# Cluster similarities with the tokens as stationary operand, and the softmax reciprocals turned in another step

## The chip, the cores and the metric

The kernel runs on one core of one Trainium2 chip. The metric is the device time of one execution in microseconds (us). The engines run at the same time, each through its own queue in program order: TensorE (PE in the profile, its loads of stationary operands PEld), VectorE (DVE), ScalarE (ACT), GpSimd (POOL) and SyncE (SP), which here only issues DMAs. They wait for each other through semaphores.

## The reference

An attention in which a query sees the keys of its own cluster alone, and two dense layers behind it:

```python
B, H, S, D = 2, 8, 768, 64          # 16 centroids a head
q_assign = argmax(q_n @ c_n)        # cluster of each query, by normalised centroids
k_assign = argmax(k_n @ c_n)        # cluster of each key
mask   = q_assign[:, :, :, None] == k_assign[:, :, None, :]
scores = where(mask, q @ k.T / 8, -1e9)
attn   = softmax(scores) @ v        # then (1536, 512)
x = gelu_like(attn @ w_in) @ w_out  # 512 -> 2048 -> 512
x = relu(x @ w_in2)**2 @ w_out2     # 512 -> 2048 -> 512
```

Inputs are float32, and every product is made of float32r parts (a high and a low part), so that the argmax and the result are exact enough.

## The kernel before

**Stages.** Attention comes first, then the two dense layers. The change touches the attention alone.

**Attention.** The 16 pairs of batch and head are worked in eight groups of two heads. A head has six tiles of 128 queries, so a group has twelve steps and the main loop (L528) has 96 tiles. The loop makes the scores of a tile two steps (LEAD) before it uses them. A step of a group is numbered u = 0 to 11.

**A step** issues, in this order: the scores on PE (L346, L347: four matmuls into one of two PSUM tiles "big0", "big1"), the row maximum on DVE (L352), the turns of an older tile's exponentials on PE (L370: two halves of three transpositions into "pt0" and "pt1"), the high part of each half on ACT (L380), the low part on DVE (L383), a share of the product with v on PE (L395), the exponential on ACT (L361), and then the side work for the next group. Each engine keeps this order.

**Side work** (`side`, L500) prepares the next group while this one is worked: `split` makes high and low parts of q and k (a cast on DVE, a subtraction on POOL), `turn` transposes them on PE (L240) into the PSUM bank "sd", `turned` copies them out on ACT (L251) and sends a half to other partitions by a DMA of SP (L256). The heads of k and q are split in steps 5, 8 and 10 and in step 0, the turns stand in steps 7, 9, 10, 11 and 0 to 3. Steps 4 and 5 make the similarities, step 6 `best` and `bested`, step 7 `hot`, step 8 `rows` and `rowed`. Nearly all of this side work passes through the bank "sd".

**Similarities.** `cpad` holds the centroids' columns padded with zeros to 64 and 128, so that four accumulating matmuls (L264) give the similarities of both heads of q and k, high and low part of the centroids, as 128 rows of 384 tokens; ACT copies them out (L271), and `best` (L277) multiplies them by two stacked identities (`ident2`), which turns them to tokens by rows and adds the high and the low part. `bested` takes the maximum over the 16 clusters (L283), compares (L285), and weighs by the cluster's number (L288, on POOL); `hot` takes the maximum again (L294) and compares (L296, `hot_n`), so that the first of equal clusters wins. `rowed` sends the result to the operands of the scores by eight DMAs of SP (L322).

**Reciprocals.** After a group's last exponential `recip` (L423, L424) inverts the sums on DVE. `recip_rows` then transposes them on PE into "sd" (L429), DVE copies them out (L431, `rows`), and SP writes them to DRAM (L433). `spread` (L440) reads them back by two DMAs, each row on 64 partitions, and `norm` (L446) multiplies the group's result with them on POOL. They stand in step 0, step 2 and step 7 of the next group.

**Queues.** SP issues its DMAs in program order, about 0.6 us each, POOL works `split`'s low parts, `merged` (L418: adds the two halves of a product when their DMA has landed), `vals` and `norm` in program order.

Of the kernel before, what the change touches and what calls it, by code (L numbers as in the profile page):

```python
# [10 lines left out]
F32 = mybir.dt.float32  # L11
# [20 lines left out]
def tile_kernel(ctx, tc, q, k, v, cent, w_in1, w_out1, w_in2, w_out2, cw_cols, out):  # L32
# [101 lines left out]
    def attention(actx):  # L134
# [50 lines left out]
        cpad = one.tile([P, 2, H, 2, NS * C], F32R, name="cpad")  # L185
        nc.gpsimd.memset(f32(cpad), 0.0)

        ident2 = one.tile([P, NS * C], F32, name="ident2")
        nc.vector.tensor_copy(ident2[0:NS * C], identF[0:NS * C, 0:NS * C])
        nc.vector.tensor_copy(ident2[NS * C:], identF[NS * C:, NS * C:])  # L190
# [19 lines left out]
        def centroid_columns(c_hl):  # L210
            pc = psum([P, 2, H, C], F32R, "sd", "pc")
            for t in range(2):
                nc.tensor.transpose(pc[:, t].rearrange("p h c -> p (h c)"),
                                    c_hl[:, t].rearrange("p a d -> p (a d)"), identR)
            for x in range(2):
                for i in range(G):
                    o = C * (x * G + i)
                    nc.scalar.copy(cpad[:, x, i::G, :, o:o + C].rearrange("p h t c -> p t h c"),
                                   f32(pc[:, :, i::G, :]))


        class Prep:
# [35 lines left out]
            def sims(self, half, tag="sd"):  # L258

                self.ps = psum([P, QB], F32, tag, "ps")  # L260
                cols = slice(half * QB, (half + 1) * QB)
                both = [(x, hh) for x in (1, 0) for hh in range(G)]
                for x, hh in both:
                    nc.tensor.matmul(self.ps, cpad[:, x, self.h0 + hh].rearrange("p t c -> p (t c)"),  # L264
                                     self.__dict__["qk"[x] + "2", hh][:, cols],
                                     start=((x, hh) == both[0]), stop=((x, hh) == both[-1]))

            def simmed(self, half):
                if half == 0:
                    self.st = one.tile([P, S], F32, tag="st", name="st")  # L270
                nc.scalar.copy(self.st[:, half * QB:(half + 1) * QB], self.ps)  # L271

            def best(self):

                self.pm = psum([P, NJ, NS, C], F32, "sd", "pm")
                for j in range(NJ):
                    nc.tensor.matmul(self.pm[:, j].rearrange("p h c -> p (h c)"),  # L277
                                     self.st[:, j * P:(j + 1) * P], ident2, start=True, stop=True)

            def bested(self, start=False):  # L280
                pm = self.pm
                mx = tiny.tile([P, NJ, NS], F32, tag="mx", name="mx", bufs=1)
                nc.vector.tensor_reduce(out=mx, in_=pm, op=ALU.max, axis=AX)  # L283
                sim = one.tile([P, NJ, NS, C], F32, tag="sim", name="sim")
                nc.vector.tensor_tensor(  # L285
                    out=sim, in0=pm, in1=mx.unsqueeze(3).to_broadcast([P, NJ, NS, C]), op=ALU.is_equal)
# [177 lines left out]
        for half in range(2):  # L464
            p0.sims(half, ("sd", "pa")[half])
            p0.simmed(half)
        p0.best()
# [32 lines left out]
        def side(gn, u):  # L500
# [10 lines left out]
            elif u in (4, 5):  # L511
                pe, copy = (lambda: p.sims(u - 4)), (lambda: p.simmed(u - 4))
            elif u == 6:
                pe, copy = p.best, p.bested
            elif u == 7:
                mid = p.hot
            elif u == 8:
                pe, copy = p.rows, p.rowed
# [9 lines left out]
        for t in range(-LEAD, NTILE):  # L528
# [24 lines left out]
            if (t + LEAD) % GT == 0 and t > 0:  # L553
# [24 lines left out]
            if (t + LEAD) % GT == 2 and t > 0:  # L578
                spread((t + LEAD) // GT - 1)
            if t % GT == 5 and 0 < t // GT < NG:  # L580
# [177 lines left out]
```

## Time and profile before

| | us |
|---|---|
| median of 3 runs (820.99 to 822.8) | 822.67 |
| profiled execution | 823.47 |
| its span | 821.7 |
| PE busy in the span | 791.8 |
| DVE busy | 572.8 |
| ACT busy | 437.5 |
| POOL busy | 203.8 |

The span runs from the first instruction of the program to its last; the execution is a little longer. Busy PE time counts the pipeline of each matmul, so it does not tell what PE could do at its peak. The attention takes the first 290 us of the span, a third of it. In a list of waits a line tells which instruction had to wait, what released it, the sum, the number of such waits and the longest. In a timeline a row is an instruction, or several of one kind that follow each other; in brackets stands the idle time of the engine before it and what ended it.

### The profile page before, as it was taken

How to read it: one execution, taken by the hardware profiler on the slowest of the kernel's cores; microseconds unless marked ns; L12 is line 12 of the kernel's file. 1: busy time of each engine (PE TensorE's matmuls, PEld its weight loads, DVE VectorE, ACT ScalarE, POOL GpSimd, SP SyncE). 2: the span in 40 equal slices, each digit the busy share in tenths (PEclk: the TensorE clock that was granted, in tenths of full speed). 3: DMA queues.
4: the chain of work that ended last, by engine and by line, in shares of the span. 5: the costliest groups of instructions: out<-in, count | busy, mean ns of one | idle time of the engine just before them, and what ended most of it. 6: DMA issues, size and time to landing. Idle time of an engine off the chain costs nothing.

```text
span 821.7 us, 12438 instructions
## 1 busy us (share of the span) xinstructions
PE 791.8 (96%) x4610; PEld 696.6 (85%) x4610; DVE 572.8 (70%) x941; ACT 437.5 (53%) x925; POOL 203.8 (25%) x186
## 2 busy tenths in 40 slices
PE   5899999999998999999999999999999999999997
PEld 4789889889897888888888888878888888888886
DVE  7888798898889699999759999988322225222222
ACT  5788878888887745555535445464222224222222
POOL 3525344435336343333202233322000000000000
PEclk9799999999999999999999999999999999999999
DMA  9432523513211134444303344331000002000002
GB/s 247 138 80 71 140 45 107 138 41 112 69 35 42 44 103 128 128 129 127 104 4 115 113 129 129 119 112 52 1 0 1 1 1 77 0 1 1 1 1 77
DMA packets 40412, 60.89 MB, mean 74 GB/s; under 512 B 4224, under 2 KB 31648, under 8 KB 40352
## 3 DMA queue, kind: packets, MB, share of 16 engines
q1 hardware_dynamic: 35456, 53.03, 22.5%
q10 hardware_dynamic: 4896, 7.08, 2.6%
q8 instruction: 36, 0.59, 0.3%
q14 instruction: 24, 0.20, 0.1%
HBM read 46.18 MB, written 3.19 MB: 60 GB/s over the span
## 4 chain that ended last, share of the span: by engine, by line
PE 86%; DVE 8%; ACT 4%; issue 1%; ACTq 0%; POOL 0%; POOLq 0%; DVEq 0%
PE ph L129 32%; PE y L651 16%; PE y L642 10%; PE pa L395 6%; PE pt L370 6%; PE y L644 5%; PE ps L346 3%; PE ps L347 3%; ACT e L361 2%; DVE el L383 2%; DVE nm L352 2%; PE pt L240 2%; PE ps L264 1%; PE pm L277 1%; DVE dec L96 1%
## 5 line engine op out<-in xcount | busy, mean ns | idle before, releaser
L626 DVE TENSOR_TENSOR s<-s 128x512 f32<-128x512 f32 x64 | 36.2, 566 | 134.6 <-ACT s L625 134.6
L129 PE MATMUL ph<-xh,ih 128*128 128x512 f32 (+1 forms) x512 | 110.6, 338 | 1.4 <-ACT ih L102 1.2
L129 PE MATMUL ph<-xl,ih 128*128 128x512 f32 (+1 forms) x512 | 110.3, 337 | 0.5 <-DVE xl L117 0.4
L129 PE MATMUL ph<-xh,il 128*128 128x512 f32 (+1 forms) x512 | 109.6, 336 | 0.0
L352 DVE TENSOR_REDUCE nm<-ps 128x1 f32<-128x768 f32 x96 | 91.1, 949 | 23.4 <-PE ps L347 22.6
L630 ACT CAST gh<-s 128x512 fp32r<-128x512 f32 (+1 forms) x128 | 65.5, 512 | 75.0 <-DVE s L626 50.7
L383 DVE TENSOR_TENSOR el<-pt,eh 128x384 fp32r<-128x384 f32 x192 | 97.4, 548 | 7.4 <-ACT eh L380 6.8
L93 DVE SCALAR_TENSOR_TENSOR dec<-raw,dec 128x512 uint32<-128x512 uint32 x64 | 100.3, 1567 | 1.1
L625 ACT ACTIVATE s<-ph 128x512 f32<-128x512 f32 x64 | 31.2, 487 | 129.4 <-PE ph L129 129.4
L129 PEld LDWEIGHTS ph<-xh,ih 128*128 128x128 f32 x512 | 84.5, 188 | 17.0 <-ACT ih L102 1.9
L631 DVE TENSOR_TENSOR gl<-s,gh 128x512 fp32r<-128x512 f32 (+1 forms) x128 | 71.4, 557 | 39.4 <-ACT gh L630 39.4
L361 ACT ACTIVATE e<-ps,nm 128x768 f32<-128x768 f32 x96 | 88.4, 921 | 10.8 <-DVE nm L352 10.2
L380 ACT CAST eh<-pt 128x384 fp32r<-128x384 f32 x192 | 83.9, 493 | 19.2 <-PE pt L370 18.9
L129 PEld LDWEIGHTS ph<-xl,ih 128*128 128x128 f32 x512 | 83.3, 190 | 11.4 <-DVE xl L117 1.2
L129 PEld LDWEIGHTS ph<-xh,il 128*128 128x128 f32 x512 | 83.4, 190 | 10.0
L370 PE MATMUL pt<-identF,e 128*128 128x128 f32 x576 | 82.2, 277 | 3.8 <-DVE el L383 3.7
L103 POOL TENSOR_TENSOR il<-dec,ih 128x512 fp32r<-128x512 f32 x32 | 41.7, 1304 | 142.4 <-ACT ih L102 128.5
L79 ACT ACTIVATE dec<-raw 128x512 f32<-128x512 f32 x64 | 43.2, 676 | 61.5 <-DMA raw<-in_moe_w_out_dram 37.1
L651 PE MATMUL y<-oh,gh 128*128 128x512 f32 x192 | 75.1, 391 | 0.0
L651 PE MATMUL y<-ol,gh 128*128 128x512 f32 x192 | 75.1, 391 | 0.0
L651 PE MATMUL y<-oh,gl 128*128 128x512 f32 x192 | 74.7, 389 | 0.0
L346 PE MATMUL ps<-k,q 80*128 80x512 f32 x192 | 72.0, 375 | 1.9 <-ACT k L320 1.9
(118 smaller groups left out, 1535.7 us busy)
## 6 DMA issues: line engine op xcount, KB each, us to landing
raw<-in_moe_w_in_dram SPq DMA_DIRECT2D x32, 512.0 KB, 4.4
raw<-in_moe_w_out_dram SPq DMA_DIRECT2D x32, 512.0 KB, 3.3
k<-k SPq DMA_DIRECT2D x16, 192.0 KB, 2.8
q<-q SPq DMA_DIRECT2D x16, 192.0 KB, 2.5
rr<-row SPq DMA_DIRECT2D x16, 192.0 KB, 3.5
out_dram<-o SPq DMA_DIRECT2D x12, 256.0 KB, 2.3
both<-both SPq DMA_DIRECT2D x30, 96.0 KB, 2.1
rawk<-in_k_dram ACTq DMA_DIRECT2D x6, 384.0 KB, 3.3
```

Of the source, the lines that this page charges most:

```text
L93: nc.vector.scalar_tensor_tensor(out=t, in0=high, scalar=0xC0000000, in1=t, op0=ALU.bitwise_and, op1=ALU.bitwise_or)
L129: nc.tensor.matmul(ph, w[:, kc * P:(kc + 1) * P], xs[kc][z][:, a:a + n], start=(j == 0), stop=(j == len(terms) - 1))
L346: nc.tensor.matmul(ps[:, a:a + n], q1[0:K1, qs], k1[0:K1, a:a + n], start=True, stop=False)
L352: nc.vector.tensor_reduce(out=nm, in_=live["s", t], op=ALU.max, axis=AX, negate=True)
L361: nc.scalar.activation(e, live.pop(("s", t)), ACTF.Exp, bias=live.pop(("nm", t)), accum_out=sums[:, s:s + 1])
L370: nc.tensor.transpose(pt[:, i], e[:, kc * P:(kc + 1) * P], identF)
L380: nc.scalar.copy(place("eh", t, u), live["pt", t, u])
L383: nc.vector.tensor_tensor(out=place("el", t, u), in0=live.pop(("pt", t, u)), in1=f32(place("eh", t, u)), op=ALU.subtract)
L630: nc.scalar.copy(gh, self.s)
L631: nc.vector.tensor_sub(gl, self.s, f32(gh))
L642: nc.tensor.matmul(y[m], l[:, cs], gha if hi else gla, start=first, stop=last)
L651: nc.tensor.matmul(y[m], l[:, cs], r, start=(fc == 0 and z == 0), stop=(fc == KF - 1 and z == 2))
```

## The change

The similarities are computed with the tokens on the partitions. The 128 columns of tokens of q or k are the stationary operand, and the 16 columns of the head's centroids, high and low part side by side, stream past it: 12 matmuls of 32 columns for k in step 4 and 12 for q in step 5. ACT copies the high part's products out and DVE adds the low part's. `best`, the padded centroids, their memset and `ident2` are gone, and `bested` reads SBUF. At the start, for the first group, the same calls stand in the place of the old ones, so that the two adds come ahead of the first `decode` on DVE.

The transposition of the reciprocals with its copy and its DMA moves from step 0 to step 6, where the bank "sd" has no other use now, `spread` from step 2 to step 8, behind `rowed`, and `norm` from step 7 to step 10, behind that step's `split`. The last group's stay where they were.

```diff
-        cpad = one.tile([P, 2, H, 2, NS * C], F32R, name="cpad")
-        nc.gpsimd.memset(f32(cpad), 0.0)
-        ident2 = one.tile([P, NS * C], F32, name="ident2")
-        nc.vector.tensor_copy(ident2[0:NS * C], identF[0:NS * C, 0:NS * C])
-        nc.vector.tensor_copy(ident2[NS * C:], identF[NS * C:, NS * C:])
+        cols = one.tile([P, H, 2, C], F32R, name="cols")
...
-            for x in range(2):
-                for i in range(G):
-                    o = C * (x * G + i)
-                    nc.scalar.copy(cpad[:, x, i::G, :, o:o + C].rearrange("p h t c -> p t h c"),
-                                   f32(pc[:, :, i::G, :]))
+            nc.scalar.copy(cols.rearrange("p h t c -> p t h c"), f32(pc))
...
-            def sims(self, half, tag="sd"):
...
-            def simmed(self, half):
...
-            def best(self):
...
+            def sims(self, nm, tag="sd"):
+                self.ps = psum([P, NJ, G, 2, C], F32, tag, "ps")
+                for hh in range(G):
+                    for j in range(NJ):
+                        nc.tensor.matmul(self.ps[:, j, hh].rearrange("p t c -> p (t c)"),
+                                         self.__dict__[nm + "2", hh][:, j * P:(j + 1) * P],
+                                         cols[:, self.h0 + hh].rearrange("p t c -> p (t c)"), start=True, stop=True)
+
+            def summed(self, nm):
+                if nm == "k":
+                    self.sim = one.tile([P, NJ, NS, C], F32, tag="sim", name="sim")
+                at = G * (nm == "k")
+                dst = self.sim[:, :, at:at + G]
+                nc.scalar.copy(dst, self.ps[:, :, :, 0])
+                nc.vector.tensor_tensor(out=dst, in0=self.ps[:, :, :, 1], in1=dst, op=ALU.add)
 
             def bested(self, start=False):
-                pm = self.pm
+                sim = self.sim
...
-        for half in range(2):
-            p0.sims(half, ("sd", "pa")[half])
-            p0.simmed(half)
-        p0.best()
+        for i, nm in enumerate("kq"):
+            p0.sims(nm, ("sd", "pa")[i])
+            p0.summed(nm)
         tf = decode(*m0)
...
             elif u in (4, 5):
-                pe, copy = (lambda: p.sims(u - 4)), (lambda: p.simmed(u - 4))
+                pe, copy = (lambda: p.sims("kq"[u - 4])), (lambda: p.summed("kq"[u - 4]))
             elif u == 6:
-                pe, copy = p.best, p.bested
+                copy = p.bested
...
-            if (t + LEAD) % GT == 0 and t > 0:
+            if (t + LEAD) % GT == 6 and t + LEAD > GT or t == NTILE - LEAD:
                 recip_rows((t + LEAD) // GT - 1)
...
-            if (t + LEAD) % GT == 2 and t > 0:
+            if (t + LEAD) % GT == 8 and t + LEAD > GT:
                 spread((t + LEAD) // GT - 1)
-            if t % GT == 5 and 0 < t // GT < NG:
+            if t % GT == 8 and 0 < t // GT < NG:
                 norm(t // GT - 1)
```

## Rows read from the trace of the kernel before

**Rows 1.** The page's chain of waits: shares of the span by engine

```profile
PE 86%; DVE 8%; ACT 4%; issue 1%; ACTq 0%; POOL 0%; POOLq 0%; DVEq 0%
```

**Rows 2.** The list of waits, 21.5 to 275 us: sum, times, longest

```profile
PEld pt L240 <- issue: 9.2, 6, 1.5
...
PE pt L240 <- DVE rows L431: 7.2, 6, 1.2
```

**Rows 3.** The chain in order of time, step 0 of a group: start, length, what

```profile
120.59 0.20 DVE rows L431
```

**Rows 4.** Timeline of weight loads, one group: start, length, instruction, count, idle before

```profile
96.62 0.19 PEld L346 LDWEIGHTS ps<-k,q 80*128 80x128 f32 x1
...
101.21 0.36 PEld L264 LDWEIGHTS ps<-k,cpad 128*128 128x128 f32 x2
...
101.91 0.19 PEld L346 LDWEIGHTS ps<-k,q 80*128 80x128 f32 x1
...
103.33 1.42 PEld L277 LDWEIGHTS pm<-ident,st 128*128 128x128 f32 x12
104.67 0.19 PEld L346 LDWEIGHTS ps<-k,q 80*128 80x128 f32 x1
...
110.05 0.19 PEld L346 LDWEIGHTS ps<-k,q 80*128 80x128 f32 x1
...
111.30 0.31 PEld L370 LDWEIGHTS pt<-identF,e 128*128 128x128 f32 x3 [0.15 <-DVE el L383]
...
125.66 0.41 PEld L240 LDWEIGHTS pt<-identR,nat 128*128 128x128 f32 x3
```

**Rows 5.** Groups of weight loads, 0 to 290 us: count, busy us, mean ns, idle before

```profile
L240 PEld LDWEIGHTS pt<-identR,nat 128*128 128x128 f32 x192 | 23.4, 149 | 14.3 <-issue 9.2 <-DVE nat L233 1.4 <-POOL nat L233 1.1
L277 PEld LDWEIGHTS pm<-ident,st 128*128 128x128 f32 x96 | 12.1, 200 | 0.5 <-ACT st L271 0.5
L264 PEld LDWEIGHTS ps<-q,cpad 128*128 128x128 f32 x32 | 6.4, 206 | 0.0
```

**Rows 6.** Timeline of DVE, steps 6 to 8 of the same group

```profile
102.98 0.96 DVE L352 TENSOR_REDUCE nm<-ps 128x1 f32<-128x768 f32 x1 [0.60 <-PE ps L347]
103.86 1.01 DVE L383 TENSOR_TENSOR el<-pt,eh 128x384 fp32r<-128x384 f32 x2
...
108.36 1.09 DVE L296 TENSOR_TENSOR hot_n<-simw,fi 128x384 bf16<-128x384 f32 x1
109.38 0.95 DVE L352 TENSOR_REDUCE nm<-ps 128x1 f32<-128x768 f32 x1
```

**Rows 7.** Timeline of POOL, step 7 and the next group's step 0

```profile
107.19 1.85 POOL L446 TENSOR_TENSOR x<-x,rr 128x768 f32<-128x768 f32 x1
...
121.83 1.01 POOL L233 TENSOR_TENSOR nat<-rawq,nat 128x384 fp32r<-128x384 f32 x1 [0.36 <-DVE nat L232]
```

**Rows 8.** Timeline of the start, 1 to 19 us

```profile
1.34 1.79 DVE L173 CAST identR<-identF 128x128 fp32r<-128x128 f32 x1 [1.34 <-POOL identF masks.py:199]
...
8.44 2.34 PEld L240 LDWEIGHTS pt<-identR,nat 128*128 128x128 f32 x18 [0.73 <-DVE nat L233]
...
11.71 0.43 DVE L88 TENSOR_SCALAR dec<-dec 128x512 f32<-128x512 f32 x1
...
13.13 2.14 PEld L277 LDWEIGHTS pm<-ident,st 128*128 128x128 f32 x12
...
15.45 0.56 DVE L283 TENSOR_REDUCE mx<-pm 128x24 f32<-128x384 f32 x1 [0.86 <-PE pm L277]
...
18.70 0.56 DVE L296 TENSOR_TENSOR hot_n<-simw,fi 128x384 bf16<-128x384 f32 x1
```

**Rows 9.** Timeline of SP's issues, first and last two of `rowed`'s eight

```profile
112.00 1.34 SPq L322 DMA_DIRECT2D q<-oh  x2
...
115.93 1.23 SPq L322 DMA_DIRECT2D k<-oh  x2
```

**Rows 10.** The view of one line, L440 (`spread`): its sixteen DMAs, issue to landing

```profile
DMA to landing us min/median/max: 3.2/3.5/4.6
```

## What the change should do to the time

> **What bounds the kernel now.** I read the chain of waits first, because the shares of busy time are averages over two very different stages. It is TensorE for 86% of the span, DVE for 8% and ACT for 4% [rows 1], so only what PE waits for, or what PE itself has to do, can move the end. The change touches the first 290 us alone, in which eight groups of twelve steps run; I number the steps of a group 0 to 11 (u in the code). The second place is therefore the list of waits over that stage: PE's turn of step 0 (L240) waits for DVE's copy `rows` (L431) six times, 7.2 us by the matmul rows and 9.2 us by the weight-load rows [rows 2]. The chain shows why: the twelve columns of sums are transposed into the bank "sd", DVE empties it only after its max and its two subtractions, and PE's next user of that bank is the turn that follows in program order [rows 3]. Third, the timeline of weight loads, which gives PE's true pace: a matmul's own duration holds its pipeline, but the distance from one load to the next does not. Steps 4 to 9 start at 96.62, 99.14, 101.91, 104.67, 107.73 and 110.05 in the group I use (six starts; the first, the last and two between stand in [rows 4]); PE is dense in them but for 0.20 us in step 9, where a load waits for `el` [rows 4].
>
> **A, the moved reciprocals.** Per group the transposition and the copy go from step 0 to step 6, where the bank is free since `best` no longer uses it. The wait of 9.2/6 = 1.53 us [rows 2] goes. What is late next in step 0: DVE's `sums` still stand at the end of step 11 and hold the max back a little, but the last `el` of step 0 ends at 120.6, where the copy begins [rows 3], and the transposition that needs its bank would come at about 120.7 (the first half 0.3 earlier, its `el` ending 0.5 earlier), so nothing replaces the wait, but without room to spare. There are six such steps (the first group has no sums, the last no turn): -9.2 us. The transposition itself costs PE about 0.14 in step 6, and DVE's copy 0.2 [rows 3].
>
> **B, PE's work for the similarities.** Removed per group: 2 x 4 matmuls of 384 columns, 0.70 us for four (101.21 to 101.91), and 12 of `best`, 1.34 us for all (103.33 to 104.67) [rows 4]: 2.74. Added: 24 matmuls with 128x128 stationaries and 32 columns. No row has a 128x128 fp32r stationary with so few columns. One bound is `best`, 0.112 each, whose 64 columns are too few to explain the pace; the other is the turn, an fp32r transposition with loads of 149 ns against 200 for `best`, in proportion 0.083. The old similarities' loads, fp32r and no transposition, take 206 [rows 5], so I take the pace of `best`: 24 x 0.112 = 2.68. The Trainium skill, "TensorE: Matmul & The Clock Gate", section "LDWEIGHTS (loading the stationary operand)", has a load cost its columns over 1.2 GHz whatever streams behind it, which speaks against exchanging the operands: 128 columns are 0.107 us (an estimate from the page), 2.56 per group, early and late alike, which `best` at the start (E) did not keep; by it the whole would come to about 824.4. PE's sum hardly moves, but its place does: steps 4 and 5 grow by 0.64 each, step 6 shrinks by 1.34 - 0.14 = 1.20. Per group +0.08.
>
> **C, what this does to DVE in steps 6 to 9.** Step 6 now starts 1.28 later (103.19), step 7 only 0.08 later (104.75). DVE's subtraction of step 6 cannot start before 1.95 us into that step, as before (101.91 to 103.86) [rows 4, 6]: 105.14. It frees the second transposition bank 1.06 later, at 106.20; PE would want it 1.05 us into step 7, at 105.80. A wait of 0.40. From there to DVE's max of step 8 it was 5.52 us (103.86 to 109.38) [rows 6]. The exact-match step `hot_n` in it took 1.09 beside POOL's `norm` [rows 6, 7], and 0.56 at the start without it [rows 8]; `norm` moves from step 7 to step 10, so 0.5 goes; the copy of `rows` adds 0.2, and 0.1 of idle time goes: 5.1, so the max of step 8 starts at 110.25. In the trace the second bank of step 9 came free 1.92 after that max (109.38 to 111.30) [rows 4, 6], so now at 112.17; PE's step 9 would start at 110.53 and want it at 111.58. A wait of 0.59 where 0.20 was. Together B and C are 0.08 + 0.40 + 0.39 = 0.87 per group, for six groups, and 0.5 for the first, whose steps are longer: +5.7. The two DVE adds and ACT's smaller copies lie beside the longer steps 4 and 5: DVE was idle for 0.60 us before step 6's max [rows 6] and these steps are now longer; at nothing, but if that cover were gone, 0.3 each.
>
> **D, the queues that the moved spread passes.** The read-back of the reciprocals (`spread`, two DMAs) is now issued in step 8 behind the eight DMAs of `rowed`, and `norm` on POOL comes two steps later instead of five. The eight issues took from 112.00 to 117.16 [rows 9]; the second read-back is issued 0.6 later still, at 117.8, and lands 3.5 us on [rows 10], at 121.3. POOL is in order: `norm` waits for that, takes 1.85 [rows 7], then comes `merged` (about 1.0, as the same kind of POOL work), then the low part of q's second head (L233, 1.01) [rows 7], done at 125.1. PE wants that tile for the turn of step 2, at 125.66 now [rows 4] and 1.53 earlier with A, 124.1. A new wait of 1.0 us, which C shifts on both sides alike. Behind PE's waiting turn stand the scores of step 3. It meets the five groups that have both a norm before and a turn: +5.1. Bounds: landings were between 3.2 and 4.6 in the trace, so 0.7 to 2.1 per group, and zero if POOL has done that low part first.
>
> **E, the start.** There the chain is serial: turns, similarities, argmax, hot rows, first scores. DVE took decode and two casts, 11.71 to 14.58, while PE did similarities, and then waited 0.86 until 15.45 [rows 8]. In the new order the two adds come ahead of the decode in DVE's queue, so its 2.87 us come after them. Turns ended at 10.8; the padded centroids' memset, beside which a 128x128 cast took 1.79 [rows 8], and the two copies of `ident2` are gone, which I value at 1.1 (0.4 to 1.5). PE's pace there is uncertain: `best` took 2.14 for twelve [rows 8] against 1.34 later, the turns 0.13 each. 24 x 0.178 = 4.3 us (3.1 by the turns' pace). ACT's copy and the add have half the elements of an operation that takes 0.56 [rows 8]: 0.8 for both with PE's drain. 10.8 - 1.1 + 4.3 + 0.8 + 2.87 = 17.7 against 15.45: +2.2 (1.0 to 3.4). At the tail nothing changes: the last reciprocals stay where they were.
>
> **The sum.** -9.2 + 5.7 + 5.1 + 2.2 = +3.8. The profiled execution took 823.47 us, its span 821.7, so 827.3 on that base; the median of the three runs, 822.67, is 0.8 lower, which gives 826.5.
>
> **Rivals.** *Short loads*: the new matmuls run at the turns' pace (0.083, at the start 0.13). Steps 4 and 5 grow by 0.3 only, step 7 starts 0.5 earlier than before, B and C are 0.24 per group (1.6 in all), E is 1.0: -1.5, 821.2; it would not be slower. For it speaks that both operands are fp32r; against it the 206 ns of the old loads. It decides from a pace below about 0.10. *Loads at one pace*: the new loads keep 0.112 at the start too, E is 10.8 - 1.1 + 2.7 + 0.8 + 2.87 - 15.45 = 0.6, the sum +2.2, 824.9, within the bound. The skill's rule above would have it so; the 2.14 of `best` at the start speaks against it. *No wait on POOL*: D is zero because the read-back lands before PE gets there; -1.3, 821.4. Against it stands SP's issue time. *Both at once*: -6.6, 816.1, faster; this is the case in which only A remains. *A later read-back*: with A gone the loads of the next group (issued in step 1) come 1.5 us earlier and overlap it; a landing of 4.6 gives 2.1 per wait, +9.3, 832.0; each 0.1 us above 3.5 costs 0.5. *The change doesn't free step 0*: ahead of PE's turn the chain runs through DVE [rows 3], and if max and `el` alone hold PE there, half of A stays: +8.4, 831.1.
>
> **How the numbers follow.** The forecast with its own bounds (823.5 to 829.5) has 0.40, short loads 0.12, loads at one pace 0.10, no wait on POOL 0.17, both at once 0.08, the later read-back 0.07, step 0 not freed 0.06. About 0.3%, 2.5 us, is what a measurement of this kernel can tell from no change. Slower by more: three quarters of the forecast, 0.30, a third of the one-pace case, 0.04, and the last two, 0.13: 0.47. Faster by more: both at once, 0.08, and a quarter of short loads and of no wait, 0.08: 0.16. Within: 0.37. The range from 818.5 to 831.0 leaves out the case of both at once and part of the last two.
>
> **What would show it.** Step 0 gets shorter by about 1.5 us in six groups, and the wait for L431 is gone from the list. The weight loads of the similarities stand 0.11 apart. In the list of waits, PE's turns wait for POOL's `nat` (L233) about 1 us five times, and POOL's `norm` for the DMA `rr` several us each time; DVE's `hot_n` falls to 0.56. In the start the first `mx` comes at about 17.7. I am wrong if steps 7 and 9 keep their 3.06 and 2.53, or if `norm` does not wait.

## The result and the profile after

The changed kernel takes 831.74 us (median of four executions, 826.94 to 832.60) against 822.73 before (820.99 to 823.50): a ratio of 1.0095 [1.0074, 1.0115]. That is slower, the side the forecast leaned to, but 5 us above its 826.5 and 0.7 above the range. The profiled execution took 826.94, the fastest of the four, its span 824.7, only 3.5 us more than the profiled one before; a profile of the same kernel made later has a span of 827.8 (first experiment below). Both are needed, because part of the loss differs from one execution to the next.

The page's chain of waits, shares of the span by engine, against [rows 1]:

```profile
PE 78%; DVE 10%; ACT 3%; SPq 2%; DMA 2%; issue 2%; POOL 2%; ACTq 0%; POOLq 0%; DVEq 0%
```

PE has lost 8 points of the chain; SP's queue, a DMA and POOL stand in it now, 2% each. The list of waits over the attention stage, 21.5 to 281 us (sum, times, longest), shows why, against [rows 2]:

```profile
POOL x L434 <- DMA rr<-row: 35.4, 6, 10.3
POOL x L406 <- DMA both<-both: 22.1, 8, 3.7
...
PEld pt L358 <- DVE el L371: 11.0, 41, 0.8
...
PEld pt L231 <- POOL nat L224: 6.6, 6, 2.0
```

The wait for DVE's `rows` is gone. In its place POOL's `norm` (L434) waits for the read-back, and PE's turn (L231) for POOL's low part `nat` (L224). PE also waits longer than before (6.8 us, 17 times) for DVE's `el`. Views of one group and of the start follow, each beside its rows of before. First the weight loads from step 0 to step 3; a step is the distance from one first score load (L334) to the next:

```profile
121.00 0.19 PEld L334 LDWEIGHTS ps<-k,q 80*128 80x128 f32 x1
...
123.34 0.19 PEld L334 LDWEIGHTS ps<-k,q 80*128 80x128 f32 x1
...
125.69 0.19 PEld L334 LDWEIGHTS ps<-k,q 80*128 80x128 f32 x1
...
129.25 0.30 PEld L231 LDWEIGHTS pt<-identR,nat 128*128 128x128 f32 x3 [0.93 <-POOL nat L224]
129.50 0.19 PEld L334 LDWEIGHTS ps<-k,q 80*128 80x128 f32 x1
```

The first score loads (L346) of the same four steps in the trace of before:

```profile
117.27 0.19 PEld L346 LDWEIGHTS ps<-k,q 80*128 80x128 f32 x1
...
121.14 0.19 PEld L346 LDWEIGHTS ps<-k,q 80*128 80x128 f32 x1
...
123.49 0.19 PEld L346 LDWEIGHTS ps<-k,q 80*128 80x128 f32 x1
...
126.01 0.19 PEld L346 LDWEIGHTS ps<-k,q 80*128 80x128 f32 x1
```

Step 0 is 2.34 us long, where the trace of before has 3.87 (the wait of [rows 2, 3]); step 2 is 3.81, where it had 2.52. POOL in the same stretch, against [rows 7], and the issues of SP:

```profile
125.43 1.84 POOL L434 TENSOR_TENSOR x<-x,rr 128x768 f32<-128x768 f32 x1 [4.80 <-DMA rr<-row]
127.23 1.01 POOL L406 TENSOR_TENSOR x<-both 64x384 f32<-64x384 f32 x1
128.20 0.99 POOL L224 TENSOR_TENSOR nat<-rawq,nat 128x384 fp32r<-128x384 f32 x1
```

```profile
119.67 1.23 SPq L310 DMA_DIRECT2D k<-oh  x2
120.94 1.23 SPq L428 DMA_DIRECT2D rr<-row  x2
...
122.91 0.54 SPq L398 DMA_DIRECT2D both<-both  x1
```

The read-back leaves SP behind `rowed`'s eight issues, `norm` stands 4.80 us for it, and the low part of q ends at 129.19, when PE has waited for it. `both` leaves SP behind the read-back, which will matter. Steps 6 to 9 of the group, by weight loads and by DVE, against [rows 4, 6]:

```profile
104.78 1.48 PEld L254 LDWEIGHTS ps<-cols,q 128*128 128x128 f32 x12
106.19 0.19 PEld L334 LDWEIGHTS ps<-k,q 80*128 80x128 f32 x1
...
107.68 0.19 PEld L334 LDWEIGHTS ps<-k,q 80*128 80x128 f32 x1
...
108.70 0.31 PEld L358 LDWEIGHTS pt<-identF,e 128*128 128x128 f32 x3 [0.25 <-DVE el L371]
...
111.13 0.19 PEld L334 LDWEIGHTS ps<-k,q 80*128 80x128 f32 x1
...
113.43 0.19 PEld L334 LDWEIGHTS ps<-k,q 80*128 80x128 f32 x1
...
114.58 0.31 PEld L358 LDWEIGHTS pt<-identF,e 128*128 128x128 f32 x3 [0.39 <-DVE el L371]
```

```profile
108.10 1.01 DVE L371 TENSOR_TENSOR el<-pt,eh 128x384 fp32r<-128x384 f32 x2
109.03 0.27 DVE L419 COPY rows<-pr 12x128 f32<-12x128 f32 x1
...
112.64 0.56 DVE L284 TENSOR_TENSOR hot_n<-simw,fi 128x384 bf16<-128x384 f32 x1
113.11 0.95 DVE L340 TENSOR_REDUCE nm<-ps 128x1 f32<-128x768 f32 x1
```

In the rows left out too, DVE goes from one instruction to the next without a gap (108.10 to 116 us), and PE waits for `el` in step 7 and in step 9. From the `el` of step 6 to the max of step 8 DVE takes 5.01 us, where it took 5.52 before. The start, weight loads and DVE, against [rows 8]:

```profile
10.14 2.63 PEld L254 LDWEIGHTS ps<-cols,k 128*128 128x128 f32 x12
12.65 2.68 PEld L254 LDWEIGHTS ps<-cols,q 128*128 128x128 f32 x12
...
25.56 0.29 PEld L334 LDWEIGHTS ps<-k,q 80*128 80x128 f32 x1 [2.19 <-ACT k L308]
```

```profile
15.83 0.36 DVE L266 TENSOR_TENSOR sim<-ps,sim 128x192 f32<-128x192 f32 x1 [2.20 <-ACT sim L265]
16.11 0.42 DVE L88 TENSOR_SCALAR dec<-dec 128x512 f32<-128x512 f32 x1
...
18.89 0.54 DVE L272 TENSOR_REDUCE mx<-sim 128x24 f32<-128x384 f32 x1
```

The table below puts the spans together; every length is a difference of starts of first score loads, summed over the steps named. "Again" is the later profile of the changed kernel, "forecast" the terms A to E. The dense part runs from its first weight load (L129, at 277 us before) to the end of the span. The rest, under 0.4 us, lies in steps that are not listed.

| part of the span, us | before | after | difference | again, difference | forecast |
|---|---|---|---|---|---|
| up to the first scores | 21.73 | 25.56 | +3.83 | +2.63 | E +2.2 |
| step 0, six groups | 23.25 | 14.11 | -9.14 | -9.15 | A -9.2 |
| steps 4 to 9, first seven groups | 112.30 | 116.71 | +4.41 | +4.92 | B, C +5.7 |
| step 2, third to seventh group | 12.65 | 20.04 | +7.39 | +9.11 | D +5.1 |
| step 3 of the same | 11.81 | 11.72 | -0.09 | +1.39 | 0 |
| last group, steps 0 to 10 | 27.60 | 25.08 | -2.52 | -2.66 | 0 |
| dense part | 544.70 | 543.83 | -0.87 | +0.22 | 0 |
| whole span | 821.7 | 824.7 | +3.0 | +6.1 | +3.8 |

### The profile page after: what moved, and what is told of

Read it like the earlier page. It is cut to its first block, busy times and chain, and to the rows that moved or that the text cites. A ratio compares the mean times of both kernels' runs of the same rounds, so it can differ in the third digit from the quotient of the medians.

```text
span 824.7 us, 12495 instructions
## 1 busy us (share of the span) xinstructions
PE 796.4 (97%) x4642; PEld 697.5 (85%) x4642; DVE 565.9 (69%) x955; ACT 434.6 (53%) x922; POOL 203.4 (25%) x185
## 4 chain that ended last, share of the span: by engine, by line
PE 78%; DVE 10%; ACT 3%; SPq 2%; DMA 2%; issue 2%; POOL 2%; ACTq 0%; POOLq 0%; DVEq 0%
PE ph L129 31%; PE y L639 16%; PE y L630 11%; PE y L632 5%; PE pt L358 4%; PE pa L383 4%; DVE nm L340 3%; DVE el L371 2%; PE ps L254 2%; PE ps L334 2%; PE ps L335 2%; SPq L310 2%; DMA rr<-row 1%; ACT e L349 1%; PE pt L231 1%
## 5 line engine op out<-in xcount | busy, mean ns | idle before, releaser
L129 PE MATMUL ph<-xh,ih 128*128 128x512 f32 (+1 forms) x512 | 110.5, 338 | 1.4 <-ACT ih L102 1.2
L129 PE MATMUL ph<-xl,ih 128*128 128x512 f32 (+1 forms) x512 | 110.3, 337 | 0.4 <-DVE xl L117 0.4
L129 PE MATMUL ph<-xh,il 128*128 128x512 f32 (+1 forms) x512 | 109.6, 336 | 0.0
L129 PEld LDWEIGHTS ph<-xh,ih 128*128 128x128 f32 x512 | 84.5, 188 | 16.9 <-ACT ih L102 2.2
L349 ACT ACTIVATE e<-ps,nm 128x768 f32<-128x768 f32 x96 | 88.2, 919 | 11.2 <-DVE nm L340 11.1
L129 PEld LDWEIGHTS ph<-xl,ih 128*128 128x128 f32 x512 | 83.4, 190 | 11.3 <-DVE xl L117 1.1
L129 PEld LDWEIGHTS ph<-xh,il 128*128 128x128 f32 x512 | 83.4, 190 | 10.0
L358 PE MATMUL pt<-identF,e 128*128 128x128 f32 x576 | 84.1, 279 | 3.4 <-DVE el L371 3.2
L358 PEld LDWEIGHTS pt<-identF,e 128*128 128x128 f32 x576 | 64.8, 142 | 12.2 <-DVE el L371 11.0
L334 PE MATMUL ps<-k,q 80*128 80x512 f32 x192 | 73.0, 380 | 1.9 <-ACT k L308 1.9
```

The source lines that it names most:

```text
L129: nc.tensor.matmul(ph, w[:, kc * P:(kc + 1) * P], xs[kc][z][:, a:a + n], start=(j == 0), stop=(j == len(terms) - 1))
L334: nc.tensor.matmul(ps[:, a:a + n], q1[0:K1, qs], k1[0:K1, a:a + n], start=True, stop=False)
L349: nc.scalar.activation(e, live.pop(("s", t)), ACTF.Exp, bias=live.pop(("nm", t)), accum_out=sums[:, s:s + 1])
L358: nc.tensor.transpose(pt[:, i], e[:, kc * P:(kc + 1) * P], identF)
```

## The experiments

Two theories of the miss stand against each other at first: the wait in step 2 (D) is larger in most executions than in the profiled one (theory P in the texts below), or the start (E) is (theory Q). Behind that lie the questions of what holds step 2, what sets steps 7 and 9, and what the moved reciprocals are worth alone. "Step 2" below is its length from the third to the seventh group, one by one or summed (12.65 before), "steps 4 to 9" the length in a steady group (15.98 before).

| kernel | median us | ratio to before | first scores | step 0, six | step 2, sum of five | steps 4 to 9 |
|---|---|---|---|---|---|---|
| changed, again | 831.91 | 1.0127 [1.0099, 1.0155] | 24.36 | 14.10 | 21.76 | 16.75 |
| norm later | 831.03 | 1.0099 [1.0079, 1.0119] | 24.7 | 14.10 | 20.59 | 16.75 |
| decode first | 828.97 | 1.0075 [1.0062, 1.0089] | 22.52 | 14.11 | 22.24 | 16.75 |
| even shares | 829.15 | 1.0072 [1.0055, 1.0088] | 24.6 | 14.12 | 22.42 | 16.74 |
| read-back earlier | 822.66 | 1.0001 [0.9992, 1.0010] | 25.08 | 14.10 | 14.26 | 16.75 |
| POOL's order | 822.00 | 0.9993 [0.9984, 1.0003] | 25.13 | 14.11 | 15.36 | 16.75 |
| old reciprocals | 833.07 | 1.0123 [1.0109, 1.0137] | 24.20 | 22.98 | 13.63 | 17.08 |
| three edits | 820.12 | 0.9963 [0.9951, 0.9976] | 22.83 | 14.12 | 13.57 | 16.75 |
| rows on ACT | 818.64 | 0.9956 [0.9944, 0.9968] | 23.75 | 14.11 | 12.97 | 16.56 |
| loads later | 819.16 | 0.9960 [0.9947, 0.9972] | 21.91 | 14.11 | 12.60 | 16.75 |
| sums on POOL | 818.98 | 0.9960 [0.9948, 0.9972] | 23.2 | 14.11 | 13.45 | 16.56 |
| all edits | 818.40 | 0.9948 [0.9934, 0.9961] | 22.6 | 14.10 | 12.63 | 16.57 |

**The changed kernel again.** Unchanged.

> The changed kernel once more. Its profiled execution took 826.9 us, +3.5 on the profiled one before, and the other three 831.0 to 832.6. Theory P (read-back): the extra 4 to 6 us lie in the waits of step 2, because the landing of the read-back differs from execution to execution; then a trace of a slow execution shows step 2 at 4.6 to 5.3 us in five groups instead of 3.6 to 4.4, and the same start. Theory Q (start): they lie before the second group, where TensorE runs at its lower clock level; then step 2 stays at 3.6 to 4.4 and the first group, 31.8 us in the profiled execution, or the start ahead of it, 25.6 us, is longer by about 5.

The start is 1.2 us shorter here than in the first profile, and the span still 3.1 longer. The largest difference is the third group, 3.3 us: step 2 took 5.96 (4.08 in the first profile), and step 3, where nothing waits, 3.78 instead of 2.35. The dense part adds 1.1. Two stretches there, PE's gap and what follows (stretch, length, busy time of PE, weight loads, DVE, ACT and POOL, granted clock, DMA share, GB/s), and the load that ends the gap:

```profile
94.90:97.60 2.70, 0.04 (x1) 0.00 (x0) 0.94 (x2) 1.16 (x3) 1.94 (x2) 1.00 1.08 238
97.60:101.00 3.40, 3.37 (x14) 3.18 (x15) 1.12 (x2) 1.00 (x3) 0.44 (x1) 0.51 0.51 118
```

```profile
97.63 0.42 PEld L231 LDWEIGHTS pt<-identR,nat 128*128 128x128 f32 x3 [3.03 <-POOL nat L224]
```

PE stands still for 2.7 us, and the granted clock of the 3.4 us that follow is 0.51, the lower of the two levels (1.2 of 2.4 GHz). So a late tile costs here its wait and, behind it, work at the lower clock: 1.4 us in step 3 alone. The two profiles with the decode first and with even shares have the same fall behind gaps of 2.7 and 3.3 us (step 3 at 3.43 and 3.57); the one with norm later has a gap of 2.4 us in the same place and none. The mean granted clock, which is on record for each execution, goes with the time: of the ten executions of the changed kernel the first profiled one alone has 1.00 (826.94 us), those between 830.0 and 832.6 have 0.995 to 0.998, the two at 837 have 0.992 and 0.993. Once the wait of step 2 is taken away (read-back earlier, POOL's order), all twenty have 0.999 or 1.00. This speaks for theory P, though the loss lies in one group and not evenly in five: an execution differs from another by the waits of step 2 and by what the clock does behind them. Only two of the ten were traced, so the 837 are not shown to be that.

**Norm later on POOL.** What D names is taken out of the way: `norm` three steps later, behind the low part of q.

```diff
-            if t % GT == 8 and 0 < t // GT < NG:
+            if t % GT == 11 and 0 < t // GT < NG:
```

> The changed kernel with norm three steps later (step 1 of the next group but one instead of step 10), so that POOL has made the low part of q's second head before it waits for the read-back. My theory of term D: the waits of PE's turn for POOL in step 2 go, step 2 falls from 3.6 to 4.4 to 2.5 in five groups, 7.4 us in all by the profiled execution: 819.5 on its base, 824.3 on the median's. Theory P: the scatter goes as well, all executions near 819.5. Theory Q: one execution in four near 819.5, the others near 825. Rival: the wait moves to PE's step 4 or to the next group's side work behind the late norm on POOL; then less than half of 7.4 comes back.

Step 2 stays at 5.71, 3.47, 3.55, 3.97 and 3.89. POOL in the third group:

```profile
96.00 0.98 POOL L406 TENSOR_TENSOR x<-both 64x384 f32<-64x384 f32 x1 [8.53 <-DMA both<-both]
96.96 0.98 POOL L224 TENSOR_TENSOR nat<-rawq,nat 128x384 fp32r<-128x384 f32 x1
97.91 1.82 POOL L434 TENSOR_TENSOR x<-x,rr 128x768 f32<-128x768 f32 x1
```

`norm` no longer stands ahead of the low part of q, and next to nothing is won (0.9 us, the intervals overlap): `merged` (L406) does, and waits 8.53 us for its own transfer. That transfer leaves SP at 90.82, behind the eight issues of `rowed` and the two of the read-back, and takes 5.05 us to land where the median of all thirty is 2.3. So D had the right tile and the right engine, and half of the cause.

**The read-back earlier.** `spread` one step earlier, ahead of `rowed`'s eight issues.

```diff
-            if (t + LEAD) % GT == 8 and t + LEAD > GT:
+            if (t + LEAD) % GT == 7 and t + LEAD > GT:
```

> The changed kernel with the read-back (spread) issued one step earlier, so that its two DMAs stand on SP's queue ahead of rowed's eight; norm and merged stay where they are on POOL. Read-back theory (norm waits because rr is issued behind the eight DMAs): norm finds rr landed, step 2 of groups 2 to 6 comes from 5.96, 4.06, 3.83, 3.88, 4.03 (the changed kernel run again) down to 2.5 to 2.8 us, step 3 of group 2 from 3.78 to 2.35, and the time is 831.9 - 9.5 = 822.4. Rival, POOL's order (whatever stands ahead of the low part of q on POOL and waits for a DMA holds it: with norm freed, merged waits for its own transfer of both, which still leaves behind rowed's eight): step 2 stays at 3.4 to 4 us, the time is 827 to 830.

The time is that of the kernel before, 1.0001 of it. POOL in the third group:

```profile
87.74 1.84 POOL L434 TENSOR_TENSOR x<-x,rr 128x768 f32<-128x768 f32 x1
```

`norm` finds `rr` landed: the row has no idle time before it. Step 2 is 3.03, 2.93, 2.87, 2.91 and 2.52: 7.5 us less than in the changed kernel again, and step 3 of the third group is 2.34 again. `merged` is freed by the same edit: in this trace no `both` takes more than 3.2 us to land (5.1 with norm later). My rival for this run, that `merged` would hold POOL just as long, fell.

**POOL's order.** No DMA is moved; `merged` goes one step later and `norm` three, so that the low part of q stands behind nothing that waits for a DMA.

```diff
-            if blk > 1 and part == 0:
+            if blk > 1 and part == 1:
...
-            if t % GT == 8 and 0 < t // GT < NG:
+            if t % GT == 11 and 0 < t // GT < NG:
```

> The changed kernel with POOL's order changed and no DMA moved: merged one step later (part 1 instead of 0) and norm three steps later, so that nothing that waits for a DMA stands ahead of the low part of q's second head. Theory POOL's order: PE's turn of step 2 finds nat ready, step 2 is 2.5 to 2.7 us in every group, the granted clock stays at 1.0 there, and the time is 831.9 - 10 = 821.9, although read-back and both land no sooner. Rival, the transfers themselves (scores of the next steps wait for the k and q copies that land late in the same crowd): step 2 or 3 keeps a wait, now for a DMA, and the time is above 827.

822.0 us, as the theory had it, though the read-back and `both` land no sooner (medians 3.8 and 2.5 us). POOL in the fourth group:

```profile
124.24 1.01 POOL L224 TENSOR_TENSOR nat<-rawq,nat 128x384 fp32r<-128x384 f32 x1 [4.10 <-PE pt L358]
126.12 0.99 POOL L406 TENSOR_TENSOR x<-both 64x384 f32<-64x384 f32 x1 [0.86 <-ACT eh L368]
```

The low part is done at 125.25 and PE's turn waits for it nowhere. Step 2 was expected at 2.5 to 2.7 and is 3.89, 3.06, 2.97, 2.91 and 2.53: what is left is a wait for DVE's `el` behind a late `eh` of ACT, and the loads-later run comes back to it. With this run and the one before, the wait in step 2 is priced on the medians: 9.9 and 9.3 us of the changed kernel's 831.9.

**The old reciprocals.** The new similarities stay, the transposition and copy go back to step 0, the read-back to step 2, `norm` to step 7.

```diff
-            if (t + LEAD) % GT == 6 and t + LEAD > GT or t == NTILE - LEAD:
+            if (t + LEAD) % GT == 0 and t > 0:
...
-            if (t + LEAD) % GT == 8 and t + LEAD > GT:
+            if (t + LEAD) % GT == 2 and t > 0:
...
-            if t % GT == 8 and 0 < t // GT < NG:
+            if t % GT == 5 and 0 < t // GT < NG:
```

> The changed kernel with the reciprocals' three parts put back where the kernel before has them (transpose and rows in step 0, read-back in step 2, norm in step 7); the similarities stay new. What the move is worth: step 0 back from 2.35 to 3.88 in six groups (+9.2), step 2 back to 2.53 (-9.1 in groups 2 to 6 and -1.4 in step 3 of group 2), step 7 the same or up to 0.5 longer each (hot beside norm on POOL, 1.09 for 0.60). If the move gives back what it gains: 831.9 - 1.3 = 830.6, up to 833 with step 7. As the prediction had it (a gain of 9.2 against 5.1 lost): 836. If the late low part of q has another cause than the move (the new similarities): step 2 keeps 3.8 to 4.1 and the time is 840 or more.

833.07 us, 1.2 above the changed kernel: with its delayed tile the move is worth next to nothing, and with POOL's order mended 833.07 - 822.00 = 11.1. The similarities by themselves cost 10.6 against the kernel before, on the medians. The profiled execution, whose span is 8.3 longer than that of before, has 1.1 more in steps 4 to 9 of six groups (0.3 in the first), 2.5 at the start and 1.0 in one step 2, and 2.2 less elsewhere, 1.4 of it in the dense part. Steps 7 and 8 are longer than in the changed kernel (3.56 and 2.59), since DVE's exact match is back beside `norm`:

```profile
112.90 1.08 DVE L284 TENSOR_TENSOR hot_n<-simw,fi 128x384 bf16<-128x384 f32 x1
```

**Even shares.** Are steps 7 and 9 long because PE has too little in step 6? The first block's products are shared out evenly over the steps.

```diff
-        AV_CUTS = ((0, 4, 4, 12), (0, 4, 8, 12), (0, 4, 8, 12), (0, 5, 9, 12))
+        AV_CUTS = ((0, 4, 8, 12), (0, 4, 8, 12), (0, 4, 8, 12), (0, 5, 9, 12))
```

> The changed kernel with the product with v dealt evenly over steps 5, 6 and 7 (4, 4, 4 matmuls instead of 4, 0, 8). My theory of term C: PE's waits of step 7 (0.40) and step 9 (0.34 above before) come from the short step 6, which DVE cannot follow; with 0.7 us moved from step 7 into step 6 both go: steps 6 to 9 fall from 10.12 to about 9.4 in each of seven groups, 5 us in all. Rival: DVE's work between step 6 and step 8 is itself the bound, whatever PE's shares are: steps 6 to 9 keep 10.1 within 0.2 and the time does not change by more than 1.

Steps 6 to 9 are 2.18, 2.36, 2.67 and 2.90 instead of 1.49, 3.45, 2.30 and 2.89: 10.11 against 10.13. The work moved and the sum did not, so it isn't PE's share in a step that sets it; my theory fell and the rival held for the steps. The median is 2.8 below the changed kernel's, for which the trace shows no cause (its own execution took 830.4, step 2 of the third group 6.42). Two of the four executions have a mean granted clock of 1.00, against one of ten of the changed kernel; why stays open.

**Rows on ACT.** On the kernel of the three edits (below), the copy of the turned reciprocals leaves DVE.

```diff
-            nc.vector.tensor_copy(rows, pr)
+            nc.scalar.copy(rows, pr)
```

> The kernel of the three edits (820.1) with the copy of the turned reciprocals, 0.27 us in step 6, on ACT instead of DVE. If DVE's own work from step 6 to step 8 sets the length of steps 7 to 9 (DVE stands without a gap from 108 to 116 us in the changed kernel): steps 7 to 9 lose 0.2 to 0.3 us in six groups, 8.64 to about 8.4, and the time is 820.1 - 1.5 = 818.6. If PE or a chain behind hot_n sets it: steps 7 to 9 stay at 8.64 and the time at 820.1.

DVE's max for step 8 comes 0.2 sooner behind the `el` of step 6, and its 0.27 us are gone from between (left out: the maximum and match of step 6, the next `nm` and `el`, and the second maximum with the exact match). In the changed kernel it was 5.01 us from the one row to the other, here it is 4.83:

```profile
105.27 1.01 DVE L371 TENSOR_TENSOR el<-pt,eh 128x384 fp32r<-128x384 f32 x2
...
110.10 0.95 DVE L340 TENSOR_REDUCE nm<-ps 128x1 f32<-128x768 f32 x1
```

Step 9 falls from 2.89 to 2.70, step 7 stays at 3.45. DVE's run from step 6 to step 8 is thus the bound of step 9. That step 7 hangs on the `el` of step 6, ahead of that run, fits this and C; no run tests it by itself. 818.64 is 1.5 below the three edits, and the intervals overlap.

**Sums on POOL.** On the kernel with the rows on ACT, ACT copies both parts of the similarities out of PSUM into a new tile `two` and POOL adds them, but for the first group.

```diff
...
-                nc.vector.tensor_tensor(out=dst, in0=self.ps[:, :, :, 1], in1=dst, op=ALU.add)
+                nc.gpsimd.tensor_tensor(out=dst, in0=two[:, :, :, 0], in1=two[:, :, :, 1], op=ALU.add)
...
```

> The kernel with the rows' copy on ACT, and besides the sums of the similarities on POOL: ACT copies both parts out of PSUM (128x384) and POOL adds them, so that DVE loses 0.36 us in step 4 and in step 5. If DVE's work is the bound of steps 4 to 9: steps 7 and 9 come back to the 3.06 and 2.53 us of the kernel before, 0.5 to 0.7 us a group in all, -3 to -4 us: 815 to 816. If what bounds is the work between step 6 and step 8 alone (the adds of steps 4 and 5 lie in gaps that DVE has there): no more than the kernel with the rows on ACT, 818.6. If POOL's slower add makes the maxima of step 6 late: step 7 grows by 0.5 us a group and the time is 821 to 822.

818.98 us, steps 7 and 9 at 3.45 and 2.70 as without it. 0.72 us of DVE's work a group is gone and buys nothing: the adds of steps 4 and 5 lay beside longer steps, as the prediction costed them.

**Decode first.** At the start, the first decode ahead of the similarities in DVE's order.

```diff
         m0 = magnitude(raw[0])
+        tf = decode(*m0)
         for i, nm in enumerate("kq"):
...
-        tf = decode(*m0)
```

> The changed kernel with the first decode ahead of the similarities in program order at the start, so that DVE does it while PE makes them. My theory of term E: first scores start at 25.6 in the changed kernel and 21.7 before; the queue order is worth the 2.3 us that the decode stood between the second add and the first max, so the first scores start at about 23.3 and the time falls by 2.3. Rival (PE's clock alone): the similarities on PE end no earlier and the rest of the chain hides the decode, less than 0.8. Theory Q says that the scatter of 5 us changes or goes when the start is moved; theory P says that it stays.

First scores at 22.52, 1.8 and 3.0 us sooner than in the two profiles of the changed kernel. All six kernels of the table with the decode first have theirs between 21.9 and 23.8 us, all seven profiles of the new similarities without it between 24.2 and 25.6. The median is 2.9 lower, though by itself it prices nothing: even shares, which leaves the start alone, is as low. DVE there:

```profile
10.34 0.43 DVE L88 TENSOR_SCALAR dec<-dec 128x512 f32<-128x512 f32 x1
...
15.05 0.36 DVE L266 TENSOR_TENSOR sim<-ps,sim 128x192 f32<-128x192 f32 x1 [2.11 <-ACT sim L265]
...
15.86 0.55 DVE L272 TENSOR_REDUCE mx<-sim 128x24 f32<-128x384 f32 x1
```

The maximum follows 0.8 behind the second add instead of 3.1; the decode lies beside PE's similarities again.

**Three edits.** The read-back earlier, `merged` one step later, the decode first.

```diff
         m0 = magnitude(raw[0])
+        tf = decode(*m0)
...
-            if blk > 1 and part == 0:
+            if blk > 1 and part == 1:
...
-            if (t + LEAD) % GT == 8 and t + LEAD > GT:
+            if (t + LEAD) % GT == 7 and t + LEAD > GT:
```

> The changed kernel with the read-back one step earlier, merged one step later, and at the start the first decode ahead of the similarities. If the waits of step 2 were POOL's order behind late transfers, and the start's loss the decode behind the second add: step 2 at 2.5 to 2.7 us (-10), the start 2 to 3 us shorter, 831.9 - 12.5 = 819.4, faster than the kernel before by about 0.4%. If only one of the two edits on step 2 works: 823 to 826. If neither: 829, as with the decode alone.

820.12 us, faster than both kernels, and 0.4% below the one before. The gains of step 2 and of the start add up to within 0.7 us of the forecast.

**Loads later.** Besides the three edits, ACT issues the next group's loads in step 2. In the changed kernel it issues them in step 1, and the `eh` of step 2 stands behind the last of them (the 0.76 is put down to PE, whose turn had been done since 124.99):

```profile
125.04 0.55 ACTq L157 DMA_DIRECT2D rawv<-in_v_dram  x1
...
125.63 0.86 ACT L368 CAST eh<-pt 128x384 fp32r<-128x384 f32 x2 [0.76 <-PE pt L358]
```

```diff
-            if u == 1 and gn + 1 < NG:
+            if u == 2 and gn + 1 < NG:
```

> The kernel of the three edits with the loads of the next group's k, q and v issued by ACT in step 2 instead of step 1. If what is left of step 2's wait (2.91, 2.56, 2.59 and 2.99 us against 2.53, and 2.43 against 2.35 in step 1) is ACT held by the issue of loads while the transfers are dense: steps 1 to 3 lose 1.0 to 1.3 us in all, and the time is 820.1 - 1 = 819. If the loads come too late for DVE's high part of the next k in step 5 (they took 5 to 9 us to land in the changed kernel): steps 5 and 6 grow by 0.5 to 1 us a group and the time is 823 or more.

Step 2 is 2.52 or 2.53 in every group, which settles what was left there: ACT, held while it issues loads, had made `eh` late. Step 1 keeps its 2.42, and steps 5 and 6 do not grow. 819.16 is 1.0 below the three edits, and the intervals overlap.

**All edits.** The rows on ACT and the later loads together.

```diff
+            if u == 2 and gn + 1 < NG:
...
+            nc.scalar.copy(rows, pr)
```

> The three edits, the rows' copy on ACT and the loads in step 2 together. If their gains are of different places (steps 1 to 3 and step 9) they add: step 2 at 2.53, step 9 at 2.70 us, 820.1 - 1.0 - 1.2 = 817.9. If one takes the other's place (ACT, which makes the rows' copy and issues the loads, or DVE next in line): 818.6 to 819.2, as each alone.

Both effects stand in the trace (2.53 in step 2, 2.70 in step 9). The time, 818.40 us, is the lowest of all, 0.9948 [0.9934, 0.9961] of the kernel before, but 0.2 and 0.8 under the two with one edit each, so the times don't show that the gains add.

## Why the prediction was right or wrong

**The step that failed is D, the price of the new wait in step 2; that the first profile came out near the sum is luck.** Forecast +3.8 of span, measured +3.0 and, in the later profile, +6.1. In the +3.0 D and E are 3.9 us above their forecast, B and C 1.3 below, and the last group and the dense part, which the sum put at nothing, 3.4 below. The execution is also the one of ten whose mean granted clock is 1.00. So the last step failed with D: from one profiled execution the sum was carried to the median by the kernel's own offset, as if a new wait came out alike each time. This one doesn't.

**A held.** Six times 1.52 instead of 1.53; nothing took the place of the wait.

**B held, and with it the choice of pace in the steady groups.** The twelve new loads of a step take 1.41 us up to the score load behind them (104.78 to 106.19), 0.112 us apart but for the first; that was the value taken from `best`. Steps 4 and 5 grew by 0.69 and 0.62. Short loads, the rival, is out. The other rival about loads has them at one pace also at the start: there they stand 0.21 apart (twelve from 10.14 to 12.65). The Trainium skill, "TensorE: Matmul & The Clock Gate", section "LDWEIGHTS (loading the stationary operand)", has a load cost its columns over 1.2 GHz, 0.107 us for 128 (an estimate from it); the steady groups agree within 5%, the start does not.

**C held.** Steps 7 and 9 grew by 0.40 and 0.34 (forecast 0.40 and 0.39), DVE's run from the `el` of step 6 to the max of step 8 came out at 5.01 (forecast 5.1), and the two small terms beside them (adds at nothing, the copy of `rows` at 0.2) were measured: nothing and 0.19. My later reading, that the short step 6 causes both waits, fell with the even shares. The first group, costed at 0.5, got 0.2 shorter in one profile and 0.3 longer in the other: its step 6 of before, 3.51 long, had more to give.

**D is the term that was mis-sized: 5.1 was forecast, 9 to 10 was measured** (9.9 and 9.3 on the medians, 7.4 and 10.5 in the two profiles). The chain was the right one: read-back behind `rowed`, POOL in order, low part of q late, PE's turn. By the list of waits in the five steps 2, PE's turn waits for POOL's low part 6.0 us in the first profile and 8.0 in the later one. The rest was missing from the term: PE waits for `el` behind ACT, held by the issue of loads (1.6 and 1.2 us), and in the later profile step 3 runs at the lower clock (1.4).

What makes POOL later than forecast stands in its rows: `norm` starts 4.2 to 5.0 and 4.0 to 5.5 us behind the start of step 0, where the prediction has 4.0, 0.6 late on average in both: in some groups the read-back leaves SP up to 0.5 later, in others more time passes from its issue to `norm`. `merged` was costed as 1.0 us of work, though it waits for a transfer of its own that leaves SP behind the same ten issues; that wait adds 1.4 us in the later profile and nothing in the first, but holds POOL in full when `norm` is taken away.

The rival "a later read-back" has the 832.0 that came, at a chance of 0.07, but only in part for its reason: it needs every landing at 4.6, so `norm` 1.1 late, and the landings that the two traces hold for these groups are 3.4 to 3.8, where [rows 10] have 3.5 in the middle. What landed later are the loads of the next group and, at times, `both` (up to 4.9 us against 3.5 before). The bounds of 0.7 to 2.1 per group held in four groups of five; the third, with up to 3.4 and the clock behind it, is outside.

**E is mis-sized too: +2.2 forecast, +3.8 and +2.6 measured.** In the first profile the maximum came at 18.89 instead of 17.7: similarities 5.2 us instead of 4.3 (0.21 a load for 0.178), turns done at 10.1 instead of 9.7, and the decode behind the adds as forecast (2.8). The rest, 0.4, is slower DVE work behind it. The 0.178 was a mean over two paces: one by one, the twelve loads of `best` in the trace of before stand 0.21 apart up to 14.5 us and 0.11 from there, and at 14.5 us that trace's record of the granted clock begins, with 1.00. The new loads are all as slow as the first ones. (The record in the changed kernel's first profile begins at 35.4 us, so the 1.00 that a view prints for its start is no measurement.) The later profile is 1.2 shorter ahead of the similarities: their first load comes at 8.94 instead of 10.14. The decode's place is the cause of most of the loss and is shown by its run.

**What the sum left out** is a gain: the last group is 2.5 us shorter. There DVE decodes weights while POOL splits x, and before, `norm` stood among it. The sum has no term for it. The first and the last of DVE's four decode steps, before, then after:

```profile
253.51 1.92 DVE L88 TENSOR_SCALAR dec<-dec 128x512 f32<-128x512 f32 x1
...
262.01 2.30 DVE L96 SCALAR_TENSOR_TENSOR dec<-raw,dec 128x512 uint32<-128x512 uint32 x1
```

```profile
259.90 0.97 DVE L88 TENSOR_SCALAR dec<-dec 128x512 f32<-128x512 f32 x1
...
267.31 0.67 DVE L96 SCALAR_TENSOR_TENSOR dec<-raw,dec 128x512 uint32<-128x512 uint32 x1
```

L96 took 2.30 while POOL ran `norm` from 261.93, and 0.67 with `norm` gone to the group's first third; steps 7 and 8 are 1.7 us shorter. With the old reciprocals back it is 2.30 again. L88 took 1.92 beside the whole of POOL's split `xl`, and 0.97 where `norm`, now ahead of the splits, had put them at another place against DVE's steps; step 5 is 0.9 shorter. L96 has the same effect as `hot_n`'s 1.09 against 0.56 [rows 6, 7], which the prediction used in step 7 and did not look for in the last group. The Trainium skill, "SBUF — State Buffer", section "Who interferes with whom", says that a DVE instruction with two inputs in SBUF contends with a POOL instruction that reads SBUF; the rows of L96 and `hot_n` agree.

**Open:** why the third group is hit harder than the others, why the granted clock fell there in three profiles and not in a fourth, what the two executions at 837 us did, and why the start differs by 1.2 us between two executions. The dense part's 0.9 between the two first profiles has no cause that I could show; the later one has 0.2 the other way.

## What to carry to other kernels

When a transfer is moved to a later place in a queue, list every waiter on the in-order engine behind it, not only the one that uses it: here a second waiter, whose transfer stood in the same queue, kept nearly the whole wait when the first was taken away. Putting the work that TensorE needs ahead of the work that waits for DMAs gave back 9.9 us, as much as the move had earned in step 0 (9.15). And a wait that depends on how transfers meet isn't priced by one execution: profile the changed kernel twice before a median is explained.

## What the runs showed of the hardware

- A TensorE that stood 2.7 us came back at a granted clock of 0.51 for 3.4 us; the score load there took 0.29 to 0.34 us instead of 0.19. In two more profiles, where it stood 2.7 and 3.3 us, the clock fell 1.2 to 1.3 us after it had come back; in a fourth it stood 2.4 us and the clock did not fall.
- 128x128 fp32r stationaries that aren't transposed load 0.112 us apart in the steady groups and 0.21 apart between 10 and 15 us. `best`'s twelve at the start of the kernel before change from 0.21 to 0.11 at 14.5 us.
- The loads of the next group (384 KB each) took 5.3 us to land for k and 7.5 for v (medians) against 3.3 and 5.1 before, when the read-back, the copies and the loads were issued within 5 us. `both` (96 KB) took up to 3.9, 4.9, 5.1 and 5.3 (first profile, again, norm later, POOL's order), against a median of 2.3 and at most 3.5 before; the landings of the read-back on record there are 3.4 to 3.9, against 3.3 to 4.6 before.
- DVE work with two inputs in SBUF beside POOL's 1.84 us `norm` took 2.30 against 0.67 (128x512) and 1.08 against 0.56 (128x384).
